# Three edits of order in a fused attention, MLP and soft-MoE kernel: slot sums one step later, running sums behind the exponentials, splits behind the copy of the global keys

## The chip, the cores and the metric

The kernel runs on one core of a Trainium2 chip. The metric is device microseconds of one execution, as the median of several runs. Engines are named as in the profile: PE is TensorE (PEld its weight loads), DVE is VectorE, ACT is ScalarE, POOL is GpSimd, SP is SyncE, whose queue issues the DMAs. A line such as L587 is line 587 of the kernel's source.

## The reference, cut to what matters

```python
# attention: B 4, H 8, S 768, D 64; 8 global keys, a local band of 96
scores = scale * q @ k.T + bias            # bias: -slope * distance
scores = where(is_global | is_local, scores, -1e9)
a = exp(scores - max); a = a / (sum(a) + 1e-9)
x = (a @ v)                                # -> 3072 tokens x 512
# MLP
h = x @ w_in                               # 512 x 2048
x = (h * sigmoid(h)) @ w_out               # 2048 x 512
# soft MoE, 8 experts x 4 slots
logits = x @ phi                           # 3072 x 32
d = exp(logits - logits.max(0)); d /= d.sum(0) + 1e-9
slot_input = d.T @ x                       # 32 slots, sums over all 3072 tokens
slot_out = relu(slot_input @ w1[e]) @ w2[e]
c = softmax(logits, 1)
out = c @ slot_out
```

## The kernel before, in words

The 3072 tokens are 24 tiles T of 128, six to a batch entry (t = T % 6). Three tiles make a chunk c, so there are eight chunks. For each chunk TensorE does two long layers: 16 steps f of layer 1 (`l1_step`, L499 to L501) and 12 quarter steps of layer 2 (`l2_part`, L519 to L521). Nearly every operand is kept as a high and a low fp16 part, so that a product takes three matmuls; `hi` (L199 on ACT, L201 on POOL, L203 on DVE) writes a high part and `lo` (L207, L209) a low one.

While chunk c is in these layers, the attention of the next chunk's tiles is fed in between the steps, from a list of items that `other_items` writes out. For a tile T these are: `s_step(T, pr)` for four pairs of heads (scores, L314 or L324; softmax on DVE L329 and ACT L330), `pv_step(T - 1, half)` (probabilities times values, L369), `split(T + 1)` (the high and low parts of the next tile's q, k and v), `load(T + 2)`. `slot_end` deals the items out evenly over the chunk's first 23 of 28 slots, one slot after each step of the layers.

Two places matter here. The first is the keys' ring `kr` of four tiles: after the scores of tile T are done, its first 8 columns are overwritten with the global keys (`hi("P", kr[:, :, :, u, 0:8], kg, 0)`, POOL, 16x8 elements a partition, tiles with 1 <= t < 5), so that the scores of tile T + 1 find them there. The second is the online soft-max over tokens, a chain that runs one chunk behind: `logits` (L541), `slots1` (transpose L555, maximum L557, L558), `slots2` (maximum of all tokens L565, L568 to L573, then `e16`, the exponentials' high part L203 and low part L209) and `slots3`, which sums the tokens into the slots on TensorE (L585, L587, L589), scales the running sums `acc` and `ssum` by `alpha` (L590, L591) and adds (L593, L594). Each is put off by a number of layer steps with `at(lag, ...)`.

In the first stage (to about 160 us) the MLP's weights are also converted from fp32 pieces to two fp16 parts (`conv`: L459, L461, L466, L469, L479, L487); tiles 0 to 5 go there in another layout (`paired`).

The order in which an engine runs its instructions is not the program's: a list scheduler sets it from its own costs, with the program's order as priority and data dependences as bounds. `tc.issue_after(ins)` adds an edge: what the block traces on the engine of `ins` stands behind `ins` on that engine.

Of the kernel before, what the change touches and what calls it, by code (L numbers as in the profile page):

```python
# [12 lines left out]
ALU = mybir.AluOpType  # L13
# [7 lines left out]
NS = NE * SPE  # L21
# [9 lines left out]
NTILE = NT // 128  # L31
# [3 lines left out]
CT, C0 = max(CHUNKS), CHUNKS[0]  # L35
first = [sum(CHUNKS[:c]) for c in range(NCH)]
chunk_of = {first[c] + i: (c, i) for c in range(NCH) for i in range(CHUNKS[c])}
# [8 lines left out]
def p2(e):  # L46
    return float(2.0 ** e)
# [44 lines left out]
XTE = 'VDA'  # L92
GLE = 'VVVVVVVVVVVVVVVV'
GATE = {1: (0, 0), 2: (0, 1), 3: (1, 0), 4: (1, 1), 5: (2, 0), 6: (2, 1)}
CFG = dict(phi="P", plo="P", xhi="A", xlo="P", ghi="A", lag_l=5, lag_s=2, tail_slots=5)
C4E = "PPPPPPPP"
CTE = "AVAVAVAV"

# [1 line left out]
def fast_kernel(tc, keepp, q_l, k_l, v_l, q_f, k_f, n_global, n_local, w_in, w_out, phi, w1, w2, shapes, pick_c, out):  # L100


    nc = tc.nc
    V, A, G = nc.vector, nc.scalar, nc.gpsimd
# [4 lines left out]
    with ExitStack() as ctx:  # L109
# [87 lines left out]
        def hi(eng, out, in_, e):  # L197
            if eng == "A":
                A.activation(out=out, in_=in_, func=AF.Copy, scale=p2(e))  # L199
            elif eng == "P":  # L200
                G.tensor_scalar(out=out, in0=in_, scalar1=p2(e), scalar2=0.0, op0=ALU.mult, op1=ALU.add)  # L201
            else:
                V.tensor_scalar(out=out, in0=in_, scalar1=p2(e), scalar2=None, op0=ALU.mult)  # L203

        def lo(eng, out, in_, e, h):
            if e == 0:
                (V if eng == "V" else G).tensor_tensor(out=out, in0=in_, in1=h, op=ALU.subtract)  # L207
            else:
                V.scalar_tensor_tensor(out=out, in0=in_, scalar=p2(e), in1=h, op0=ALU.mult, op1=ALU.subtract)  # L209

        def absmax(col, in_, axis=AX.X):
            V.tensor_reduce(out=smp[:, col:col + 1], in_=in_, axis=axis, op=ALU.max, apply_absolute_value=True)
# [26 lines left out]
        def at(lag, fn):  # L239
            seq[0] += 1  # L240
            heapq.heappush(heap, (now[0] + lag, seq[0], fn))
# [5 lines left out]


        staged = {}

        def paired(T):

            return T < NPAIR
# [15 lines left out]
        def split(T):  # L269
# [21 lines left out]
            if t == 2:  # L291
                absmax(T // TPB, v16[:, u, 0:2, 0], AX.XY)

        def s_step(T, pr):
            t, u = T % TPB, T % NR
            w = 128 if t == 0 else 256
# [34 lines left out]
            if pr == 3 and 1 <= t < TPB - 1:  # L331
                if paired(T):
                    hi("P", kr32[:, 0, 0:4, u, 0:8], kg32, 0)
                else:
                    hi("P", kr[:, :, :, u, 0:8], kg, 0)
            if lp == 1:
                pb, ptb = p16[half], pt[half].rearrange("p z h s c -> p (z h s) c")
                if t == 0:
# [18 lines left out]
        def pv_step(T, half):  # L357
# [13 lines left out]
            if half == 1:  # L371
                if 1 <= t < TPB - 1:
                    if paired(T):
                        V.tensor_copy(out=v16[0:8, u], in_=vg[0:8])
                    else:
                        hi("P", v16[0:8, u], vg[0:8], 0)
                if t == TPB - 2 and T + 2 < NTILE:
                    hi("P", vg[0:8], v16[0:8, (T + 2) % NR], 0)
                ri = rinv[T % 2]
                V.tensor_scalar(out=ri, in0=psum_[T % 2], scalar1=1e-9, scalar2=None, op0=ALU.add)  # L380
                V.reciprocal(out=ri, in_=ri)
                V.tensor_tensor(out=x1f, in0=o, in1=ri.rearrange("p (h o) -> p h o", o=1).to_broadcast([128, H, D]), op=ALU.mult)
                xb = x16[T % 2]
                x1v = x1f.rearrange("p h d -> p (h d)")
                c, i = chunk_of[T]
                xv = xt[c][:, :, :, 128 * i:128 * i + 128]
                if T < C0 and XTE[T] != "D":
                    flip(xv[:, 0], xv[:, 1], x1v, XTE[T])
                else:
                    hi(CFG["xhi"], xb[:, 0], x1v, 0)  # L390
                    lo("V" if paired(T) else CFG["xlo"], xb[:, 1], x1v, 0, xb[:, 0])
                    nc.sync.dma_start_transpose(out=xv.rearrange("p z c t -> p (z c) t"), in_=xb.rearrange("p z f -> p (z f)"))

        def first_items():
            items = []
# [17 lines left out]
        def other_items():  # L413
            items, mark = [], {}
            for T in range(C0, NTILE):
# [2 lines left out]
                    items.append(lambda T=T: pv_step(T - 1, 0))  # L418
                items.append(lambda T=T: s_step(T, 1))
                if T + 1 < NTILE:  # L420
                    items.append(lambda T=T: split(T + 1))
                if T + 2 < NTILE and not paired(T + 2):
                    items.append(lambda T=T: load(T + 2, stage_m))
                items.append(lambda T=T: s_step(T, 2))
                if T > C0:
                    items.append(lambda T=T: pv_step(T - 1, 1))
                    mark[T - 1] = len(items)
                items.append(lambda T=T: s_step(T, 3))
                if paired(T + 2):
                    items.append(lambda T=T: load(T + 2, None))  # L430
            items.append(lambda: pv_step(NTILE - 1, 0))
            items.append(lambda: pv_step(NTILE - 1, 1))
            mark[NTILE - 1] = len(items)
            return items, [0] + [mark[first[c] + CHUNKS[c] - 1] for c in range(1, NCH)]

# [125 lines left out]
        def slots2(c):  # L561
# [10 lines left out]
            A.activation(out=l, in_=l, func=AF.Exp)  # L572
            A.activation(out=alpha, in_=alpha, func=AF.Exp)  # L573
            hi("V", e16[:, 0:nt, 0], l, E_E)
            lo("V", e16[:, 0:nt, 1], l, E_E, e16[:, 0:nt, 0])
            at(CFG["lag_s"], lambda: slots3(c))

        def slots3(c):
            nt = CHUNKS[c]
# [7 lines left out]
                        mm(both[:, k], w, e16[:, m], start=(i == 0), stop=(i == 2 * nt - 1))  # L587
            for m in range(nt):
                mm(both[:, 4], ones16, e16[:, m], start=(m == 0), stop=(m == nt - 1))  # L589
            V.tensor_tensor(out=acc, in0=acc, in1=alpha.rearrange("p (o s) -> p o s", o=1).to_broadcast([128, 4, NS]), op=ALU.mult)  # L590
            V.tensor_tensor(out=ssum, in0=ssum, in1=alpha, op=ALU.mult)  # L591
            for y in range(2):
                V.tensor_tensor(out=acc, in0=acc, in1=both[:, 0:4, y], op=ALU.add)  # L593
                V.tensor_tensor(out=ssum, in0=ssum, in1=both[:, 4, y], op=ALU.add)  # L594
# [722 lines left out]
```

## Time and profile before

| | |
|---|---|
| median of 3 runs | 744.09 us (741.79 to 746.35) |
| the profiled execution's own time | 742.64 us |
| its span, first to last instruction | 740.9 us |
| granted TensorE clock, mean | 0.983 |
| busy: PE, DVE, ACT, POOL | 682.3, 463.2, 325.4, 236.5 us |
| DMA | 120.07 MB, mean 162 GB/s |

Busy times are sums over the span; an engine's share says little by itself, since the stages differ. TensorE is the engine that is nearly always busy, so a microsecond in which it waits is read first, then who ended that wait. Matmul rows overlap: the distance from one row's start to the next is the time that it takes from the engine, the row's own duration is longer.

### The profile page before, as it was taken

How to read it: one execution, taken by the hardware profiler on the slowest of the kernel's cores; microseconds unless marked ns; L12 is line 12 of the kernel's file. 1: busy time of each engine (PE TensorE's matmuls, PEld its weight loads, DVE VectorE, ACT ScalarE, POOL GpSimd, SP SyncE). 2: the span in 40 equal slices, each digit the busy share in tenths (PEclk: the TensorE clock that was granted, in tenths of full speed). 3: DMA queues.
4: the chain of work that ended last, by engine and by line, in shares of the span. 5: the costliest groups of instructions: out<-in, count | busy, mean ns of one | idle time of the engine just before them, and what ended most of it. 6: DMA issues, size and time to landing. Idle time of an engine off the chain costs nothing.

```text
span 740.9 us, 13574 instructions
## 1 busy us (share of the span) xinstructions
PE 682.3 (92%) x5175; PEld 390.1 (53%) x5175; DVE 463.2 (63%) x1143; ACT 325.4 (44%) x864; POOL 236.5 (32%) x215
## 2 busy tenths in 40 slices
PE   3789888799999999999999899999999999999993
PEld 2445443345645655566556555665566545665352
DVE  4999889986852887288528872786277216504232
ACT  6868665545522553165215531653155214302121
POOL 0000104530561567135716572356143400300000
PEclk9999898999999999999999999999999999999997
DMA  6998667833563656544635656445224794384997
GB/s 205 270 283 261 138 140 191 268 121 75 108 150 75 110 130 136 121 86 114 143 72 119 125 126 131 86 104 125 58 44 66 172 332 145 124 350 188 380 366 245
DMA packets 165240, 120.07 MB, mean 162 GB/s; under 512 B 143920, under 2 KB 150448, under 8 KB 159152
## 3 DMA queue, kind: packets, MB, share of 16 engines
q1 hardware_dynamic: 165168, 119.13, 60.3%
q8 instruction: 42, 0.69, 0.4%
q14 instruction: 30, 0.25, 0.1%
HBM read 79.01 MB, written 6.29 MB: 115 GB/s over the span
## 4 chain that ended last, share of the span: by engine, by line


## 5 line engine op out<-in xcount | busy, mean ns | idle before, releaser
L201 POOL TENSOR_SCALAR arena<-arena 128x1024 f16<-128x1024 f32 (+5 forms) x127 | 124.3, 991 | 291.1 <-ACT arena L330 111.5
L499 PE MATMUL bank<-rows,arena 128*128 128x384 f16 x512 | 169.1, 331 | 0.8 <-ACT rows L199 0.7
L500 PE MATMUL bank<-rows,arena 128*128 128x384 f16 x512 | 168.9, 330 | 0.0
L501 PE MATMUL bank<-rows,arena 128*128 128x384 f16 x512 | 168.4, 330 | 0.0
L199 ACT ACTIVATE arena<-bank 128x384 f16<-128x384 f32 (+1 forms) x153 | 77.4, 506 | 170.5 <-DVE bank L505 98.2
L330 ACT ACTIVATE arena<-arena 128x256 f32<-128x256 f32 (+1 forms) x192 | 92.2, 482 | 94.9 <-DVE arena L329 93.9
L519 PE MATMUL bank<-arena 128*128 128x512 f16 x336 | 127.0, 383 | 1.9 <-ACT arena L479 1.9
L520 PE MATMUL bank<-arena 128*128 128x512 f16 x336 | 127.6, 380 | 0.5 <-DVE arena L487 0.5
L521 PE MATMUL bank<-arena 128*128 128x512 f16 x336 | 127.5, 380 | 0.0
L209 DVE SCALAR_TENSOR_TENSOR arena<-bank,arena 128x384 f16<-128x384 f32 (+2 forms) x154 | 87.9, 571 | 31.8 <-ACT arena L199 30.7
L207 POOL TENSOR_TENSOR arena<-arena 128x1024 f16<-128x1024 f32 (+1 forms) x45 | 89.7, 1993 | 19.7 <-ACT arena L199 16.7
L329 DVE CUSTOM_DVE_ANT_0 arena<-bank,arena 128x256 f32<-128x256 f32 (+1 forms) x192 | 70.4, 395 | 40.6 <-PE bank L324 36.8
L505 DVE SCALAR_TENSOR_TENSOR bank<-arena,bank 128x384 f32<-128x384 f32 x128 | 71.4, 558 | 32.1 <-ACT arena L503 30.9
L207 DVE TENSOR_TENSOR arena<-arena 128x1024 f16<-128x1024 f32 (+2 forms) x50 | 66.4, 1327 | 14.4 <-POOL arena L201 11.8
L503 ACT ACTIVATE arena<-bank 128x384 f32<-128x384 f32 x128 | 61.8, 483 | 20.0 <-PE bank L501 19.7
L501 PEld LDWEIGHTS <-arena 128*128 128x128 f16 x512 | 50.5, 99 | 34.3 <-issue 1.5
L499 PEld LDWEIGHTS <-arena 128*128 128x128 f16 x512 | 50.7, 99 | 31.3 <-issue 3.6
L500 PEld LDWEIGHTS <-arena 128*128 128x128 f16 x512 | 50.6, 99 | 29.9 <-issue 2.8
L521 PEld LDWEIGHTS <-arena 128*128 128x128 f16 x336 | 32.9, 98 | 39.8 <-issue 0.7
L519 PEld LDWEIGHTS <-arena 128*128 128x128 f16 x336 | 33.0, 99 | 37.4 <-issue 3.6
L520 PEld LDWEIGHTS <-arena 128*128 128x128 f16 x336 | 32.9, 98 | 35.0 <-issue 0.7
L369 PEld LDWEIGHTS <-arena 128*128 128x128 f16 x1056 | 40.1, 102 | 15.6 <-DMA arena<-arena 7.2
(178 smaller groups left out, 786.2 us busy)
## 6 DMA issues: line engine op xcount, KB each, us to landing
arena<-in_w_dram SPq DMA_DIRECT2D x31, 1024.0 KB, 8.4
arena<-in_k_l_dram SPq DMA_DIRECT2D x18, 512.0 KB, 4.3
arena<-in_q_l_dram SPq DMA_DIRECT2D x18, 512.0 KB, 4.1
arena<-in_w_in_dram SPq DMA_DIRECT2D x8, 1024.0 KB, 5.7
arena<-in_w_out_dram SPq DMA_DIRECT2D x8, 1024.0 KB, 5.7
arena<-in_v_l_dram SPq DMA_DIRECT2D x24, 256.0 KB, 3.0
out_dram<-arena SPq DMA_DIRECT2D x6, 768.0 KB, 4.6
arena<-in_q_f_dram SPq DMA_DIRECT2D x6, 256.0 KB, 4.7
```

Of the source, the lines that this page charges most:

```text
L199: A.activation(out=out, in_=in_, func=AF.Copy, scale=p2(e))
L201: G.tensor_scalar(out=out, in0=in_, scalar1=p2(e), scalar2=0.0, op0=ALU.mult, op1=ALU.add)
L207: (V if eng == "V" else G).tensor_tensor(out=out, in0=in_, in1=h, op=ALU.subtract)
L209: V.scalar_tensor_tensor(out=out, in0=in_, scalar=p2(e), in1=h, op0=ALU.mult, op1=ALU.subtract)
L330: A.activation(out=pw, in_=pw, func=AF.Exp, scale=-1.0, bias=nmx[:, T, h:h + 1], accum_out=psum_[T % 2][:, h:h + 1])
L499: mm(hp, wh, x[:, 0, k], start=(k == 0), stop=False)
L500: mm(hp, wh, x[:, 1, k], start=False, stop=False)
L501: mm(hp, wl, x[:, 0, k], start=False, stop=(k == 3))
L505: V.scalar_tensor_tensor(out=hp, in0=th, scalar=1.0, in1=hp, op0=ALU.add, op1=ALU.mult)
L519: mm(op, gh, woh[:, f, 0], start=(f == 0), stop=False)
L520: mm(op, gh, woh[:, f, 1], start=False, stop=False)
L521: mm(op, gl, woh[:, f, 0], start=False, stop=(f == 15))
```

## The change

`slots3` is put off by three layer steps in place of two (`lag_a`); the two DVE scalings of the running sums are queued behind the low part of the exponentials; on POOL, x's low part (tiles from 6 on) and all that `split` traces there are queued behind the latest traced copy of the global keys; x's low part and its transposing DMA become an item of their own, `pv_rest`, behind `s_step(T, 3)`.

```diff
-CFG = dict(..., lag_l=5, lag_s=2, tail_slots=5)
+CFG = dict(..., lag_l=5, lag_s=2, lag_a=3, tail_slots=5)
...
+        glob_part, slot_part = [None], [None]
+        def behind_glob():
+            return tc.issue_after(glob_part[0].ins) if glob_part[0] is not None else ExitStack()
...
+        def split_behind(T):
+            with behind_glob():
+                split(T)
...
-                    hi("P", kr[:, :, :, u, 0:8], kg, 0)
+                    glob_part[0] = hi("P", kr[:, :, :, u, 0:8], kg, 0)
...
                     hi(CFG["xhi"], xb[:, 0], x1v, 0)
-                    lo("V" if paired(T) else CFG["xlo"], xb[:, 1], x1v, 0, xb[:, 0])
-                    nc.sync.dma_start_transpose(out=xv..., in_=xb...)
+                    if paired(T):
+                        pv_rest(T)
+        def pv_rest(T):
+            c, i = chunk_of[T]
+            xb, x1v, xv = ...
+            with behind_glob():
+                lo("V" if paired(T) else CFG["xlo"], xb[:, 1], x1v, 0, xb[:, 0])
+            nc.sync.dma_start_transpose(out=xv..., in_=xb...)
...
-                    items.append(lambda T=T: split(T + 1))
+                    items.append(lambda T=T: split_behind(T + 1))
...
                     items.append(lambda T=T: pv_step(T - 1, 1))
+                items.append(lambda T=T: s_step(T, 3))
+                if T > C0:
+                    if not paired(T - 1):
+                        items.append(lambda T=T: pv_rest(T - 1))
                     mark[T - 1] = len(items)
-                items.append(lambda T=T: s_step(T, 3))
...
-            lo("V", e16[:, 0:nt, 1], l, E_E, e16[:, 0:nt, 0])
-            at(CFG["lag_s"], lambda: slots3(c))
+            slot_part[0] = lo("V", e16[:, 0:nt, 1], l, E_E, e16[:, 0:nt, 0])
+            at(CFG["lag_a"], lambda: slots3(c))
...
-            V.tensor_tensor(out=acc, in0=acc, in1=alpha..., op=ALU.mult)
-            V.tensor_tensor(out=ssum, in0=ssum, in1=alpha, op=ALU.mult)
+            with tc.issue_after(slot_part[0].ins):
+                V.tensor_tensor(out=acc, in0=acc, in1=alpha..., op=ALU.mult)
+                V.tensor_tensor(out=ssum, in0=ssum, in1=alpha, op=ALU.mult)
```

No instruction is added or taken away; a chunk in the middle has 27 items in place of 24 for its 23 slots, and its list now ends behind `s_step(T, 3)` of the next chunk's first tile. On TensorE, from chunk 2 to 5, the matmul L565 and the slot sums had steps f = 8 and 9 of layer 1 between them, with one score block and one block of probabilities times values; now it is f = 8, 9 and 10 with the same two blocks. In chunks 1, 6 and 7 too one step of layer 1 more stands there. The score blocks of pair 3 of one tile and pair 0 of the next had one step of the layers between them, and now have two.

First place: POOL, around the copy of the global keys in the middle of the kernel. 128x16x8 is that copy, 128x8x128 the high part of k, 128x8x64 that of v, 8x1024 the copy of the global values, L207 128x512 x's low part, L207 128x1024 the probabilities' low part; of the rows L201 128x1024 the first behind the copy of the global keys is the high part of q, and the next that of the probabilities. Before:

```order
L201 TENSOR_SCALAR arena<-arena 8x1024
L207 TENSOR_TENSOR arena<-arena 128x512
L201 TENSOR_SCALAR arena<-arena 128x8x128
L201 TENSOR_SCALAR arena<-arena 128x16x8
L201 TENSOR_SCALAR arena<-arena 128x1024
```

Now:

```order
L201 TENSOR_SCALAR arena<-arena 8x1024
L201 TENSOR_SCALAR arena<-arena 128x16x8
L207 TENSOR_TENSOR arena<-arena 128x512
L201 TENSOR_SCALAR arena<-arena 128x1024
L201 TENSOR_SCALAR arena<-arena 128x8x128
L201 TENSOR_SCALAR arena<-arena 128x1024
L201 TENSOR_SCALAR arena<-arena 128x8x64
L207 TENSOR_TENSOR arena<-arena 128x1024
```

The copy of the global keys has moved ahead of x's low part and of k's high part; the high part of q, which had only the copy directly ahead of it, now has the copy and x's low part ahead.

Second place: DVE, in front of the exponentials' low part in chunk 4. L568 (L588 of the new source) are the three maxima behind TensorE's L565, L571 (L591 new) the subtraction ahead of the exponentials, L203 and L209 128x3x32 their high and low part, L209 128x8x64 v's low part, L590 and L591 (L611 and L612 new) the scalings of the running sums. Before:

```order
L569 TENSOR_TENSOR arena<-arena 128x32
L571 TENSOR_TENSOR arena<-arena 128x96
L209 SCALAR_TENSOR_TENSOR arena<-arena 128x8x64
L203 TENSOR_SCALAR arena<-arena 128x3x32
L590 TENSOR_TENSOR arena<-arena 128x128
L209 SCALAR_TENSOR_TENSOR arena<-arena 128x3x32
```

Now:

```order
L589 TENSOR_TENSOR arena<-arena 128x32
L591 TENSOR_TENSOR arena<-arena 128x96
L209 SCALAR_TENSOR_TENSOR arena<-bank_73,arena 128x384
L338 ISA arena<-bank_70,arena 128x256
L338 ISA arena 128x1
L203 TENSOR_SCALAR arena<-arena 128x3x32
L209 SCALAR_TENSOR_TENSOR arena<-arena 128x8x64
L209 SCALAR_TENSOR_TENSOR arena<-arena 128x3x32
L525 SCALAR_TENSOR_TENSOR bank_74<-arena,bank_74 128x384
L611 TENSOR_TENSOR arena<-arena 128x128
L612 TENSOR_TENSOR arena<-arena 128x32
```

The scalings have gone behind the low part, and a layer 1 low part and a softmax pass (L338, L329 before) have come in ahead of it.

Third place: DVE, a little earlier in the same chunk, ahead of the three maxima. L207 64x1024 is q's low part and L207 128x8x128 k's, both of tile 18; L505 (L525 new) and L209 128x384 belong to layer 1. Before:

```order
L329 ISA arena<-bank_70,arena 128x256
L329 ISA arena 128x1
L209 SCALAR_TENSOR_TENSOR arena<-bank_75,arena 128x384
L568 TENSOR_TENSOR arena<-bank_77,arena 128x32 x2
L505 SCALAR_TENSOR_TENSOR bank_76<-arena,bank_76 128x384
```

Now:

```order
L338 ISA arena<-bank_71,arena 128x256
L338 ISA arena 128x1
L207 TENSOR_TENSOR arena<-arena 64x1024
L209 SCALAR_TENSOR_TENSOR arena<-bank_75,arena 128x384
L525 SCALAR_TENSOR_TENSOR bank_76<-arena,bank_76 128x384
L588 TENSOR_TENSOR arena<-bank_77,arena 128x32
L207 TENSOR_TENSOR arena<-arena 128x8x128
L209 SCALAR_TENSOR_TENSOR arena<-bank_76,arena 128x384
```

The low parts of the next tile's q and k now stand directly ahead of and among the maxima; they wait for the high parts that POOL writes in the first place's row.

## Rows read from the trace of the kernel before

**Rows 1.** Waits of PE, whole span: who ended them, us in total, times, longest.

```profile
PE bank L587 <- DVE arena L209: 6.5, 4, 1.9
...
PE bank L324 <- POOL arena L201: 1.6, 1, 1.6
```

**Rows 2.** Busy time by stretch: PE, PEld, DVE, ACT, POOL, then PEclk, DMA share, GB/s.

```profile
320.00:380.00 60.00, 58.54 (x463) 34.67 (x461) 41.08 (x106) 27.19 (x79) 30.10 (x23) 1.00 0.52 113
```

**Rows 3.** PE in order of time, the slot sums: start, us, [idle before <- who ended it].

```profile
263.37 0.19 PE L587 MATMUL bank<-arena 128*128 128x64 f16 x1 [1.69 <-DVE arena L209]
...
405.04 0.36 PE L565 MATMUL bank<-arena 96*128 96x96 f32 x2
...
412.36 0.19 PE L587 MATMUL bank<-arena 128*128 128x64 f16 x1 [1.92 <-DVE arena L209]
```

**Rows 4.** DVE in order of time, from the maxima to the exponentials' low part.

```profile
406.71 0.40 DVE L568 TENSOR_TENSOR arena<-bank,arena 128x32 f32<-128x32 f32 x2
...
408.12 0.68 DVE L382 TENSOR_TENSOR arena<-bank,arena 128x512 f32<-128x512 f32 x1
...
410.22 1.08 DVE L590 TENSOR_TENSOR arena<-arena 128x128 f32<-128x128 f32 x1
411.22 1.09 DVE L209 SCALAR_TENSOR_TENSOR arena<-arena 128x96 f16<-128x96 f32 x1
...
556.52 0.28 DVE L590 TENSOR_TENSOR arena<-arena 128x128 f32<-128x128 f32 x1
556.72 0.25 DVE L209 SCALAR_TENSOR_TENSOR arena<-arena 128x96 f16<-128x96 f32 x1
```

**Rows 5.** PE in order of time, one step of layer 1 between two blocks of logits.

```profile
171.07 0.32 PE L499 MATMUL bank<-rows,arena 128*128 128x384 f16 x1
...
173.01 0.38 PE L541 MATMUL bank<-arena 128*128 128x64 f16 x8
```

**Rows 6.** PE in order of time, the score block that waits for POOL.

```profile
208.87 0.60 PE L324 MATMUL bank<-arena 128*128 128x256 f16 x4 [1.59 <-POOL arena L201]
```

**Rows 7.** POOL in order of time, around copies of the global keys.

```profile
205.96 1.58 POOL L207 TENSOR_TENSOR arena<-arena 128x512 f16<-128x512 f32 x1 [2.67 <-ACT arena L199]
207.52 4.29 POOL L201 TENSOR_SCALAR arena<-arena 128x1024 f16<-128x1024 f32 x4
...
409.55 1.60 POOL L207 TENSOR_TENSOR arena<-arena 128x512 f16<-128x512 f32 x1 [1.82 <-ACT arena L199]
```

**Rows 8.** POOL and DVE by line and shape: times, busy us, mean ns.

```profile
L201 POOL TENSOR_SCALAR arena<-arena 128x1024 f16<-128x1024 f32 x66 | 81.9, 1244 | 159.5 <-ACT arena L330 89.4 <-PE bank L324 47.2 <-issue 12.0
L207 POOL TENSOR_TENSOR arena<-arena 128x512 f16<-128x512 f32 x15 | 20.4, 1357 | 17.2 <-ACT arena L199 16.7
L201 POOL TENSOR_SCALAR arena<-arena 128x128 f16<-128x128 f16 x15 | 4.4, 296 | 22.2 <-PE bank L324 15.0 <-DVE arena L207 7.2
L207 DVE TENSOR_TENSOR arena<-arena 64x1024 f16<-64x1024 f32 x18 | 27.0, 1502 | 4.1 <-POOL arena L201 3.7
```

**Rows 9.** DVE in order of time, a softmax pass, layer 1's and q's low part.

```profile
390.22 0.42 DVE L329 CUSTOM_DVE_ANT_0 arena<-bank,arena 128x256 f32<-128x256 f32 x1
...
390.56 0.56 DVE L209 SCALAR_TENSOR_TENSOR arena<-bank,arena 128x384 f16<-128x384 f32 x1
391.56 1.22 DVE L207 TENSOR_TENSOR arena<-arena 64x1024 f16<-64x1024 f32 x1 [0.44 <-POOL arena L201]
```

**Rows 10.** PE in order of time, waits that ended with a DMA.

```profile
170.84 0.39 PE L541 MATMUL bank<-arena 128*128 128x64 f16 x8 [1.51 <-DMA arena<-arena]
...
598.10 0.87 PE L369 MATMUL bank<-arena 128*128 128x64 f16 x24 [0.80 <-DMA arena<-arena]
```

**Rows 11.** PE in order of time, a wait in the weight conversion.

```profile
115.08 0.61 PE L466 MATMUL bank<-arena 128*32 128x512 bf16 x2 [3.36 <-DVE arena L381]
```

**Rows 12.** Two stretches of the weight conversion, columns as in rows 2.

```profile
88.00:92.00 4.00, 3.94 (x20) 1.95 (x21) 3.49 (x9) 2.31 (x8) 0.18 (x1) 0.51 0.34 86
...
112.00:116.00 4.00, 0.92 (x3) 0.23 (x4) 4.00 (x8) 1.39 (x2) 4.00 (x3) 0.50 0.12 45
```

More of the change, by code (lines that the diff above doesn't have):

```diff
@@ L94 @@
 GATE = {1: (0, 0), 2: (0, 1), 3: (1, 0), 4: (1, 1), 5: (2, 0), 6: (2, 1)}
-CFG = dict(phi="P", plo="P", xhi="A", xlo="P", ghi="A", lag_l=5, lag_s=2, tail_slots=5)
+CFG = dict(phi="P", plo="P", xhi="A", xlo="P", ghi="A", lag_l=5, lag_s=2, lag_a=3, tail_slots=5)
 C4E = "PPPPPPPP"
@@ L200, in hi @@
             elif eng == "P":
-                G.tensor_scalar(out=out, in0=in_, scalar1=p2(e), scalar2=0.0, op0=ALU.mult, op1=ALU.add)
+                return G.tensor_scalar(out=out, in0=in_, scalar1=p2(e), scalar2=0.0, op0=ALU.mult, op1=ALU.add)
             else:
@@ L208, in lo @@
             else:
-                V.scalar_tensor_tensor(out=out, in0=in_, scalar=p2(e), in1=h, op0=ALU.mult, op1=ALU.subtract)
+                return V.scalar_tensor_tensor(out=out, in0=in_, scalar=p2(e), in1=h, op0=ALU.mult, op1=ALU.subtract)
         def absmax(col, in_, axis=AX.X):
@@ L390, in pv_step @@
                     hi(CFG["xhi"], xb[:, 0], x1v, 0)
-                    lo("V" if paired(T) else CFG["xlo"], xb[:, 1], x1v, 0, xb[:, 0])
-                    nc.sync.dma_start_transpose(out=xv.rearrange("p z c t -> p (z c) t"), in_=xb.rearrange("p z f -> p (z f)"))
+                    if paired(T):
+                        pv_rest(T)
+        def pv_rest(T):
+            c, i = chunk_of[T]
+            xb, x1v, xv = x16[T % 2], x1f.rearrange("p h d -> p (h d)"), xt[c][:, :, :, 128 * i:128 * i + 128]
+            with behind_glob():
+                lo("V" if paired(T) else CFG["xlo"], xb[:, 1], x1v, 0, xb[:, 0])
+            nc.sync.dma_start_transpose(out=xv.rearrange("p z c t -> p (z c) t"), in_=xb.rearrange("p z f -> p (z f)"))
         def first_items():
@@ L432, in other_items @@
             items.append(lambda: pv_step(NTILE - 1, 1))
+            items.append(lambda: pv_rest(NTILE - 1))
             mark[NTILE - 1] = len(items)
@@ L589, in slots3 @@
                 mm(both[:, 4], ones16, e16[:, m], start=(m == 0), stop=(m == nt - 1))
-            V.tensor_tensor(out=acc, in0=acc, in1=alpha.rearrange("p (o s) -> p o s", o=1).to_broadcast([128, 4, NS]), op=ALU.mult)
-            V.tensor_tensor(out=ssum, in0=ssum, in1=alpha, op=ALU.mult)
+            with tc.issue_after(slot_part[0].ins):
+                V.tensor_tensor(out=acc, in0=acc, in1=alpha.rearrange("p (o s) -> p o s", o=1).to_broadcast([128, 4, NS]), op=ALU.mult)
+                V.tensor_tensor(out=ssum, in0=ssum, in1=alpha, op=ALU.mult)
             for y in range(2):
```

## The prediction

> **What bounds the kernel now.** I read the waits of TensorE over the whole span first, since it is the engine that nearly always works, then its rows in order of time around each wait, and only then the engines that ended the waits. From about 160 us to 680 us TensorE is the bound: in a stretch from the middle it is busy 58.54 of 60 us, while DVE has 41.08, ACT 27.19 and POOL 30.10 [rows 2]. What is lost there has names: the slot sums L587 wait for the exponentials' low part on DVE 6.5 us in four goes, and one score block L324 waits 1.6 us for POOL [rows 1]. The first stage, with the weights' conversion, is another matter: TensorE waits for DVE there, which has no gap (4.00 of 4 us) [rows 12].
>
> The reader should see in the third group that the slot sums of chunk 4 were wanted at 412.36 - 1.92 = 410.44 us, 5.40 us after L565 started at 405.04, and could start only at 412.36 [rows 3]. The DVE rows say why: from L568 at 406.71 to the end of the low part at 411.22 + 1.09 = 412.31 us DVE runs without a long gap, and a scaling of the running sums (L590, 1.08 us), which nobody waits for yet, lies right ahead of that low part [rows 4].
>
> **The slot sums put off by one step, and the scalings behind the low part.** One step of layer 1 is 173.01 - 171.07 = 1.94 us [rows 5]. It now lies between L565 and the slot sums, so they are wanted 5.40 + 1.94 = 7.34 us after L565. Nothing is added: TensorE does that step anyway. If the low part ended where it ends now, 412.31 - 405.04 = 7.27 us after L565, the wait would be gone by the step alone, and the scaling behind it would give another 1.0 us of room. So the edit itself is worth up to 6.5 us. But the order on DVE has changed with it, and I count that chain anew.
>
> In the new order the score block of pair 3 stands one step ahead of L565, so it ends 1.94 us before L565 starts. It releases POOL's copy of the global keys: 0.30 us. Behind that x's low part, 1.36 us by its mean, and q's high part, 1.24 us by the mean of its shape [rows 8]. That puts the end of q's high part at -1.94 + 0.30 + 1.36 + 1.24 = about 1.0 us after L565. On DVE q's low part stands ahead of the three maxima and needs that high part; queued behind it are two layer 1 operations, the maxima, k's low part and the exponentials, and TensorE's slot sums wait for the last of these. DVE should have run dry meanwhile. That such a wait happens is in the trace: q's low part waited 0.44 us for POOL at 391.56 us [rows 9], with only the copy directly ahead of q's high part; x's low part now comes on top.
>
> q's low part takes 1.22 us [rows 9] and so ends at 2.2 us, or at 2.5 with the mean of 1.50 us [rows 8]. Two layer 1 operations of 0.56 us follow [rows 9]; rows that follow each other overlap by about 0.1 us, so from start to start they are 0.47 us each. The first maximum then starts 3.1 to 3.4 us after L565; before it was 406.71 - 405.04 = 1.67 us. From there to the end of the low part it was 412.31 - 406.71 = 5.60 us. Out of that go L590 (1.00 from start to start), L382 (0.68, so 0.60) and the low part's own excess: 1.09 us beside POOL's x low part, which ran from 409.55 us with four more POOL operations behind it, against 0.25 us alone [rows 4, 7]. In come k's low part (as many elements a partition as q's, so 1.13), one layer 1 low part (0.47) and two softmax passes (0.42, so 0.34 each) [rows 9]: 5.60 - 2.44 + 2.28 = 5.44 us. The low part ends 8.5 to 8.8 us after L565, 1.2 to 1.5 us later than it is wanted. The 5.60 us hold some 0.4 us of gaps that k's low part would fill, which makes it 0.8 at best; with the low part slowed to 1.09 us again it is 2.0 to 2.3. I take a wait of **1.1 us** in place of 6.5 / 4 = 1.63, in four chunks: a gain of 4 x 0.53 = **2.1 us**, between 6.5 (the chain is short after all) and a loss of 4 x 0.67 = 2.7. I take a value near the persisting wait because every length in the chain has a row.
>
> Sharing between DVE and POOL is the weakest item. The trace shows L590 at 0.28 us alone and at 1.08 us beside POOL's operations [rows 4]. [...]
>
> **The copy of the global keys first.** The score block at 208.87 us waited 1.59 us [rows 6] for a copy behind x's low part, which ran from 205.96 us, and among the four operations from 207.52 us [rows 7]. Now the copy comes first on POOL, and two steps (3.9 us) lie between the blocks. That wait goes: **1.6 us**. The price: x's low part now waits for the score block. Its transposing DMA, and on SP's queue the loads and transposes behind it, move with it by a step at most; the next chunk's layer 1 reads x five quarter steps of layer 2 later, which covers it. Uncovered, each chunk would pay the 1.94 us of a step; I cost it at nothing. The probabilities' low part also moves back behind x's, q's, k's and v's parts on POOL, by about 1.36 + 0.7 us; its transposed copy is read some six steps later, so again nothing, and 2 us a tile if that cover were gone.
>
> **The items dealt out anew.** The last tile's second values' block L369, which waited 0.80 us for a DMA at 598.10 us, now stands four quarter steps of layer 2 behind its scores in place of three and a quarter: **0.8 us**. The three transposes ahead of the first logits no longer have a load of v directly ahead on SP's queue; L541 waited 1.51 us there [rows 10]; I take **0.5** between 0 and 1.5. In the conversion stage the order on all engines is reshuffled; DVE has the same work ahead of the last converted piece to within two softmax passes, so I take 0, with 3 us either way.
>
> **Sum.** 2.1 + 1.6 + 0.8 + 0.5 = 5.0 us. The profiled execution took 742.64 us, which gives 737.6; the median shown is 1.45 us higher, so the forecast is **739.1 us**, 0.7% faster.
>
> **The rivals.** *The slot sums' wait is gone.* For it: with the step alone the old chain would have been in time, and three of the seven slot sums wait for nothing today. Against it: the sum above. It gives 6.5 + 1.6 + 0.8 + 0.5 = 9.4 us less, **734.7**.
>
> *It does not do what it says: the wait stays as long*, because DVE now waits for q's high part instead. Gain 1.6 + 0.8 + 0.5 = 2.9: **741.2**, up to 743.9 with the 2.7 us loss. For it: the 0.44 us row; against it: DVE is idle while POOL writes x's low part and q's high part, so both can be shorter than their means, in which DVE's own work slows them.
>
> [...]
>
> **How the numbers follow.** Forecast 0.43 (its own range 736.7 to 741), wait gone 0.26, wait stays 0.19, slower 0.12. Faster by over 1%, which is below 736.65 us and about what a measurement of this kernel can tell from no change, is nearly all of the second case and a little of the first: 0.29. Slower by over 1% is two or three gaps in the conversion: 0.06. Within 1%: 0.65. The range goes from 734, which leaves out the better half of the second case, to 745, which takes in one gap and leaves out the rest: about 0.8 inside.
>
> **What would show it.** Right: L324 has no wait for POOL; L587 keeps three or four waits of about 1 us; ahead of them q's low part on DVE has an idle of 1 to 2 us ended by POOL's L201; L590's successor lies behind the low part. The second case shows L587 gone from TensorE's list. The conversion is right if TensorE's granted clock falls as often before 160 us as it did. Wrong would be a new wait of layer 1 for x, of L369 for a DMA in each tile, or a conversion stage that ends 4 us or more elsewhere than at 160 us.

## The result: 750.03 us against 743.56 us, slower

The changed kernel takes a median of 750.03 us (nine runs, 747.80 to 756.06) against 743.56 us for the kernel before on the same chip (nine, 740.65 to 746.47): 1.0100 times as long, 95% interval 1.0067 to 1.0133. The forecast was 739.1 us, the range 734 to 745. The direction was wrong, and the time lies outside the range. The profiled execution took 749.75 us with a span of 748.0 (before: 742.64 and 740.9).

Lines move with the edit: L324 is now L333, L369 is L378, L541 is L561, L565 is L585, L568 is L588, L587 is L607, L590 and L591 are L611 and L612, the loads are L271, the transposing DMAs of the probabilities, of x and of x2 are L356, L407/L408 and L552.

TensorE's waits over the whole span, the groups that answer to [rows 1] (who waited for whom, us, times, longest):

```profile
PE bank L607 <- DVE arena L209: 8.1, 4, 2.0
...
PE bank L561 <- DMA arena<-arena: 6.1, 3, 2.3
PE bank L378 <- DMA arena<-arena: 5.5, 4, 2.0
```

The scores' wait for POOL is gone from the list, as forecast. The slot sums, which were to lose 2.1 of their 6.5 us, now wait 8.1. The logits, which waited 0.8 us behind the conversion before, wait 6.1. Two of the places, TensorE in order of time ([rows 3] has the second one before):

```profile
387.00 0.39 PE L561 MATMUL bank<-arena 128*128 128x64 f16 x8 [2.28 <-DMA arena<-arena]
...
417.36 0.19 PE L607 MATMUL bank<-arena 128*128 128x64 f16 x1 [2.03 <-DVE arena L209]
```

These waits also cost clock. Stretches of the changed kernel's middle, columns as in [rows 2] (the granted clock is the third figure from the end); before, it was 1.00 in every stretch from 184 to 620 us:

```profile
380.00:440.00 60.00, 55.69 (x454) 33.89 (x453) 40.66 (x104) 26.46 (x75) 29.43 (x23) 0.94 0.48 111
...
388.00:392.00 4.00, 4.00 (x18) 2.15 (x16) 1.32 (x4) 1.09 (x4) 0.00 (x0) 0.58 0.34 66
416.00:420.00 4.00, 2.64 (x36) 1.82 (x36) 3.92 (x17) 2.34 (x6) 0.00 (x0) 0.83 0.92 179
420.00:424.00 4.00, 4.00 (x20) 2.15 (x19) 2.31 (x7) 1.59 (x5) 2.06 (x2) 0.74 0.41 155
```

TensorE is full in 388 to 392 us, yet the clock is 0.58: in quarters of a microsecond it is 0.50 from 388.00 to 391.25 us, and layer 1's matmuls start 0.32 us apart there, against 0.16 us at 1.00: 4 x 0.42 = 1.7 us lost. Three such falls, one in the stretch from 388 us, one from 416 to 424 us and one from 492 to 500 us, lose 5.1 us.

**Where the 7.1 us of span come from.** L565/L585, the slot step's first matmul, marks the chunks: the first of them stood at 183.77 us, the seventh at 625.63; now at 180.17 and 632.72, and the part behind it is the same length (115.3 us). So the conversion stage gained 3.6 us and the chunks lost 10.7. By rows: slot sums +1.6, logits 6.1 - 0.8 = +5.3, clock +5.1, scores' wait -1.6, a wait of the last tile's block of values for a DMA +0.5 (1.27 us at 600.10 us, 0.80 before), together +10.9.

**The slot sums.** VectorE, then GpSimd, ahead of the wait at 417.36 us:

```profile
408.75 2.05 DVE L207 TENSOR_TENSOR arena<-arena 64x1024 f16<-64x1024 f32 x1 [1.12 <-POOL arena L201]
...
411.76 0.18 DVE L588 TENSOR_TENSOR arena<-bank,arena 128x32 f32<-128x32 f32 x1
411.86 1.49 DVE L207 TENSOR_TENSOR arena<-arena 128x1024 f16<-128x1024 f32 x1
...
416.46 0.85 DVE L209 SCALAR_TENSOR_TENSOR arena<-arena 128x512 f16<-128x512 f32 x2
...
406.54 1.16 POOL L207 TENSOR_TENSOR arena<-arena 128x512 f16<-128x512 f32 x1
407.67 4.62 POOL L201 TENSOR_SCALAR arena<-arena 128x1024 f16<-128x1024 f32 x4
```

The second of GpSimd's four operations by itself, k's high part:

```profile
408.68 1.05 POOL L201 TENSOR_SCALAR arena<-arena 128x1024 f16<-128x1024 f32 x1
```

q's low part waits for GpSimd, as forecast, and starts 408.75 - 407.98 = 0.77 us after L585 (forecast 1.0), but takes 2.05 us, not 1.22 to 1.50: it started 0.07 us behind k's high part on GpSimd and ended 1.07 us after that ended. The row at 416.46 us holds two operations: v's low part, which stood ahead of the exponentials' high part before, and behind it the exponentials' low part that TensorE waits for.

**The logits.** VectorE with the low part of x2, GpSimd, then SP's queue, ahead of the wait at 387.00 us, changed kernel:

```profile
378.06 0.68 DVE L209 SCALAR_TENSOR_TENSOR arena<-bank,arena 128x512 f16<-128x512 f32 x1
...
378.59 2.12 POOL L207 TENSOR_TENSOR arena<-arena 128x1024 f16<-128x1024 f32 x1
...
380.73 2.97 SPq L356 DMA_TRANSPOSE arena<-arena  x1
383.75 1.30 SPq L552 DMA_TRANSPOSE arena<-arena  x1
385.15 0.53 SPq L271 DMA_DIRECT2D arena<-in_v_l_dram  x1
388.47 1.23 SPq L552 DMA_TRANSPOSE arena<-arena  x1
```

and the same place of the kernel before:

```profile
376.70 0.69 DVE L209 SCALAR_TENSOR_TENSOR arena<-bank,arena 128x512 f16<-128x512 f32 x1
...
376.66 1.23 SPq L392 DMA_TRANSPOSE rows<-rows  x1
377.94 1.34 SPq L532 DMA_TRANSPOSE arena<-arena  x1
```

The probabilities' transpose can be issued only when their low part on GpSimd ends (378.59 + 2.12 = 380.71 us). x2's transpose, for which the logits wait, stands behind it and goes at 383.75, 5.8 us later than before. Its own input was not what was late: x2's low part ended at 378.74 us (before 377.39), so the transpose stood 5.0 us for its place on the queue, 0.55 before. TensorE wanted the logits at 387.00 - 2.28 = 384.72 us.

**The conversion stage.** The gaps of 3.36 us at 115 us [rows 11] and of 3.04 us at 148.39 us are closed; the longest between 90 and 175 us is now 2.03 us. Between 20 and 184 us the granted clock fell twice in place of three times; four-microsecond stretches times (1 - clock) make 5.1 us of loss against 8.6. That this gave the 3.6 us is not shown: in e1 and e12 below the same sum is 15.4 and 13.7 us, and their first slot step stands at 183.4 and 182.5 us, no later than before. The stretch in which it was lowest now, to set beside [rows 12]:

```profile
136.00:140.00 4.00, 3.79 (x9) 1.28 (x9) 4.00 (x8) 0.50 (x2) 3.66 (x3) 0.50 0.68 242
```

### The profile page after: what moved, and what is told of

Read it like the earlier page. It is cut to its first block, busy times and chain, and to the rows that moved or that the text cites. A ratio compares the mean times of both kernels' runs of the same rounds, so it can differ in the third digit from the quotient of the medians.

```text
span 748.0 us, 13566 instructions
## 1 busy us (share of the span) xinstructions
PE 687.5 (92%) x5175; PEld 391.0 (52%) x5175; DVE 462.6 (62%) x1143; ACT 328.7 (44%) x864; POOL 241.6 (32%) x215
## 4 chain that ended last, share of the span: by engine, by line
## 5 line engine op out<-in xcount | busy, mean ns | idle before, releaser
L201 POOL TENSOR_SCALAR arena<-arena 128x1024 f16<-128x1024 f32 (+5 forms) x127 | 133.3, 1062 | 322.4 <-ACT arena L339 164.8
L541 PE MATMUL bank<-arena 128*128 128x512 f16 x336 | 128.6, 383 | 0.0
L209 DVE SCALAR_TENSOR_TENSOR arena<-bank,arena 128x384 f16<-128x384 f32 (+2 forms) x154 | 87.9, 571 | 43.2 <-ACT arena L199 42.5
L525 DVE SCALAR_TENSOR_TENSOR bank<-arena,bank 128x384 f32<-128x384 f32 x128 | 71.8, 561 | 41.4 <-ACT arena L523 40.1
L207 POOL TENSOR_TENSOR arena<-arena 128x1024 f16<-128x1024 f32 (+1 forms) x45 | 87.4, 1943 | 13.8 <-ACT arena L199 11.7
L207 DVE TENSOR_TENSOR arena<-arena 128x1024 f16<-128x1024 f32 (+2 forms) x50 | 77.4, 1549 | 20.5 <-POOL arena L201 16.2
L338 DVE CUSTOM_DVE_ANT_0 arena<-bank,arena 128x256 f32<-128x256 f32 (+1 forms) x192 | 70.2, 394 | 23.6 <-PE bank L333 20.8
L541 PEld LDWEIGHTS <-arena 128*128 128x128 f16 x336 | 33.1, 99 | 43.9 <-issue 5.3
L378 PEld LDWEIGHTS <-arena 128*128 128x128 f16 x1056 | 39.3, 101 | 18.7 <-DMA arena<-arena 9.1
```

The costliest lines, as they stand in the source:

```text
L201: return G.tensor_scalar(out=out, in0=in_, scalar1=p2(e), scalar2=0.0, op0=ALU.mult, op1=ALU.add)
L209: return V.scalar_tensor_tensor(out=out, in0=in_, scalar=p2(e), in1=h, op0=ALU.mult, op1=ALU.subtract)
L525: V.scalar_tensor_tensor(out=hp, in0=th, scalar=1.0, in1=hp, op0=ALU.add, op1=ALU.mult)
L541: mm(op, gl, woh[:, f, 0], start=False, stop=(f == 15))
```

## Experiments

The theory after the result (A): GpSimd's work behind the copy of the global keys makes the slot sums and the probabilities' transpose late. Rivals: the new dealing of items with x's DMAs (B), the slot step's own edits (C). The experiments ran in four groups, each on one chip (e1 to e4, e5 to e8, e9 to e11, e12), on which the kernel before took 741.1 to 741.8 us; each ratio is to the kernel before on the same chip. In the table "start" is the slot step of the first chunk, "length" from there to the slot step of the seventh, then what of that length TensorE's waits and the falls of the clock took (waits of under 0.5 us left out where they are no group; clock: 4 us stretches times 1 - granted clock).

| kernel | ratio to before, 95% | start | length | slot sums | logits | scores for POOL | clock |
|---|---|---|---|---|---|---|---|
| before | 1 | 183.8 | 441.9 | 6.5 | 0.8 | 1.6 | 0 |
| changed | 1.0100 (1.0067 to 1.0133) | 180.2 | 452.6 | 8.1 | 6.1 | 0 | 5.1 |
| e1 slot step alone | 1.0013 (0.9992 to 1.0034) | 183.4 | 442.5 | 0 | 0 | 5.3 | 1.7 |
| e2 all but slot step | 1.0205 (1.0162 to 1.0248) | 180.4 | 460.8 | 13.4 | 6.2 | 0 | 8.5 |
| e3 no orders behind copy | 1.0058 (1.0033 to 1.0082) | 185.3 | 440.9 | 5.4 | 1.9 | 0 | 0 |
| e4 logits six steps | 0.9901 (0.9871 to 0.9932) | 181.7 | 440.7 | 0 | 0.7 | 0 | 1.7 |
| e5 x2 from ScalarE's queue | 1.0352 (1.0314 to 1.0389) | 186.0 | 467.9 | 11.7 | 10.1 | 0 | 13.7 |
| e6 before, logits six | 0.9976 (0.9952 to 1.0000) | 178.8 | 443.8 | 0 | 0 | 7.5 | 0 |
| e7 as e3, logits six | 0.9924 (0.9898 to 0.9950) | 186.4 | 434.3 | 0 | 0 | 0 | 0 |
| e8 only split behind | 1.0086 (1.0055 to 1.0116) | 183.1 | 449.5 | 8.4 | 2.8 | 0 | 5.1 |
| e9 only x behind | 1.0164 (1.0137 to 1.0191) | 186.3 | 452.4 | 5.7 | 9.5 | 0 | 5.1 |
| e10 as e7, x of one tile behind | 0.9902 (0.9878 to 0.9927) | 184.7 | 434.3 | 0 | 0 | 0 | 0 |
| e11 as e10, old slot step | 1.0024 (1.0004 to 1.0045) | 183.7 | 444.0 | 7.6 | 0.9 | 0 | 0 |
| e12 as e10, splits to tile 10 behind | 0.9888 (0.9859 to 0.9917) | 182.5 | 438.1 | 0 | 0 | 2.4 | 0 |

In e4 3.8 us more are two waits of layer 1 for VectorE, in e12 1.1 us one. Length less all these losses is 432 to 436.5 us in all fourteen kernels, where the lengths themselves differ by 33.6 us: these waits and the clock behind them make nearly all of the difference in the chunks. Not in the columns is a wait of the last tile's block of values for a DMA, 0.8 to 3.2 us, which every kernel has once.

Start, length and waits come from one execution of each kernel. Executions of one kernel differ in their mean granted clock, 0.967 to 0.981 for the nine of the changed kernel, of which the profiled one is the highest; so the number of falls is that of the execution shown.

**e1, the slot step's edits alone in the kernel before** (`lag_a=3`, the scalings behind the low part):

```diff
-            at(CFG["lag_s"], lambda: slots3(c))
+            at(CFG["lag_a"], lambda: slots3(c))
...
+            with tc.issue_after(slot_part[0].ins):
```

> The kernel before with only the two edits of the slot step: its sums three steps behind the exponentials and its running sums scaled behind the exponentials' low part. GpSimd, the items and the DMA queue stay as before. Theory A (the part of the change that queues GpSimd's work behind the copy of the global keys is what costs): the slot sums' wait, 1.63 us at each of four chunks before, falls to 0 to 0.6, no wait of the logits for DMA and no fall of the granted clock appears between 200 and 620 us: 737 to 740 us. Rival C (the new order of the slot step itself brings the waits and the falls of the clock): the waits of the slot sums stay at 2 us, the time is 745 to 750. If one wait of a microsecond or two less gives back no time, 742 to 744.

742.03 us. The slot sums' wait went to nothing, so rival C is wrong; but no time came back. The scores' wait for the copy of the global keys took 3.7 of the 6.5 us; the rest went to the last tile's block of values, which waited 3.15 us for a DMA (0.80 before), with a fall of the clock behind it (1.7 us). e1's group for the scores' line, one more than L324, and that block's row:

```profile
PE bank L325 <- POOL arena L201: 5.3, 5, 2.0
...
597.80 1.46 PE L370 MATMUL bank<-arena 128*128 128x64 f16 x24 [3.15 <-DMA arena<-arena]
```

**e2, the changed kernel without the slot step's edits:**

```diff
-CFG = dict(..., lag_a=3, ...)
+CFG = dict(..., lag_a=2, ...)
...
-            with tc.issue_after(slot_part[0].ins):
+            with ExitStack():
```

> The changed kernel with the slot sums two steps behind and the scalings free again; only the work behind the copy of the global keys and the new items are left. Theory A: the logits' waits for DMA stay (6.1 us in three), the slot sums come one step (74 us of a chunk over 28 steps, 2.6 us) sooner than in the changed kernel while the low part that they read is as late, so they wait 3.5 to 5 us at each of four chunks in place of 2.0: 753 to 760 us. Rival C (the slot step's order costs): 743 to 746 us, waits of the slot sums near 1.6.

757.78 us, as A has it. The slot sums waited 2.75 to 2.93 us in four chunks and 2.04 us in a fifth, less than the 3.5 to 5 expected (I had taken a step at a 28th of a chunk; layer 1's is 1.94 us [rows 5]), and the clock fell five times.

**e3, the changed kernel without its two orders behind the copy:**

```diff
-            return tc.issue_after(glob_part[0].ins) if glob_part[0] is not None else ExitStack()
+            return ExitStack()
```

> The changed kernel without its two orders behind the copy of the global keys: items, place of x's low part and of its DMAs and the slot step as in the changed kernel. TensorE's order is the changed kernel's word for word. Theory A: the slot sums' wait falls from 2.0 to 0 to 0.6 us, the logits' waits for DMA from 6.1 us to at most 2, the clock stays at full speed between 200 and 620 us; the wait of tile scores for GpSimd comes back (1.6 us): 733 to 738 us. Rival B (the dealing of 27 items in place of 24 and x's DMAs behind the probabilities' DMA, not GpSimd's order, cost): the logits' waits stay at 4 to 6 us, 744 to 750 us.

745.44 us: A's time was missed, B's was met. The rows agree with neither as put: in the chunks the logits wait 1.9 us, not 4 to 6, no clock falls, and the 11.7 us that the chunks are shorter than in the changed kernel belong to the orders, as A says. But the slot sums still wait 1.4 us each, and the conversion stage is 5.1 us longer, with a wait of 3.85 us of the logits for a DMA at 171.06 us. (The profiled execution was the fastest of e3's ten, 2.3 us below their median, so its rows stand for the shape, not for the last two microseconds.) VectorE at the place shown above, e3:

```profile
407.33 1.30 DVE L207 TENSOR_TENSOR arena<-arena 64x1024 f16<-64x1024 f32 x1 [1.24 <-POOL arena L201]
...
414.62 0.24 DVE L203 TENSOR_SCALAR arena<-arena 128x96 f16<-128x96 f32 x1
414.79 0.18 DVE L390 RECIPROCAL arena<-arena 128x8 f32<-128x8 f32 x1
414.90 0.26 DVE L209 SCALAR_TENSOR_TENSOR arena<-arena 128x96 f16<-128x96 f32 x1
```

q's low part takes 1.30 us instead of 2.05. It ended at 408.63 us, 1.07 us behind the operation that GpSimd had just begun, which is a short one here:

```profile
407.26 0.30 POOL L201 TENSOR_SCALAR arena<-arena 128x128 f16<-128x128 f16 x1
```

v's low part no longer stands between the exponentials' high and low part, but that did not shorten the chain: from the first maximum to the low part's end it is 5.57 us here and 5.55 us in the changed kernel.

**e4, the logits and all behind them one step later:**

```diff
-CFG = dict(..., lag_l=5, ...)
+CFG = dict(..., lag_l=6, ...)
```

> The changed kernel with a chunk's logits, and the whole slot step behind them, one step later (six in place of five). Theory A with the DMA queue as the cause of the logits' waits: 2.6 us more room makes the three waits for DMA (2.27, 2.28, 1.58 us) vanish, and at least the fall of the clock behind the one at 387 us with them: 740 to 746 us. If the clock falls for another reason than these waits, the 5 us of its falls stay: 744 to 747. If the waits only move on to what comes next: 749 to 752.

734.36 us, better than expected: the logits' waits fell to 0.7 us, and the slot sums' waits, of which I had expected nothing, are gone too, since q's and k's low parts now stand ahead of the maxima. One fall of the clock is left, behind a wait of 2.19 us of layer 1 for VectorE.

**e5, x2's transposes from ScalarE's queue:**

```diff
-            nc.sync.dma_start_transpose(out=xtr, in_=xh...)
+            nc.scalar.dma_start_transpose(out=xtr, in_=xh...)
```

> The changed kernel with x2's transposing DMAs issued from ScalarE's queue in place of SP's; nothing else moves. Theory A (the logits wait since x2's transpose stands on SP's queue behind the probabilities' transpose, which waits for GpSimd's low part): the three waits of the logits for DMA (2.27, 2.28, 1.58 us) fall to 0.5 us together at most, the fall of the clock at 388 us goes with its wait, the slot sums' four waits of 2.0 us and the falls behind them stay: 740 to 744 us. If the DMA itself is late, because of traffic or its inputs, the logits' waits stay at 4 to 6 us: 747 to 752. If ScalarE, which then waits in its own order for VectorE's low part of x2, is what is late, the waits move to matmuls that wait for ScalarE: 748 to 756.

769.14 us, worse than any of the three. SP's queue, ScalarE's queue and TensorE in order of time:

```profile
544.33 1.80 SPq L356 DMA_TRANSPOSE arena<-arena  x1
...
548.68 1.25 ACTq L552 DMA_TRANSPOSE arena<-arena  x1
...
551.79 0.44 PE L561 MATMUL bank<-arena 128*128 128x64 f16 x8 [3.46 <-DMA arena<-arena]
```

and ScalarE's group of waits with its own issue:

```profile
ACT arena L567 <- issue: 56.6, 10, 11.6
```

x2's transpose went out 4.35 us after the probabilities' one; the median of such a DMA on SP's queue, from issue to landing, is 4.3 us, and none of the 21 transposes on ScalarE's queue was in flight together with one of SP's. So here it went out only when the other queue's transpose had landed, where on one queue it followed at once (383.75 us against 380.73 + 2.97 in the changed kernel). ScalarE stood idle ahead of such issues, 56.6 us in all in ten goes; a part of that is the wait for x2's low part, which in the go shown ended at 542.34 us, 3.96 us into an idle of 11.6. So this kernel doesn't test A's queue order: it puts a harder order in its place.

**e6, the kernel before with `lag_l=6`** (the edit of e4 alone).

> The kernel before with nothing but the logits (and the slot step behind them) one step later, six in place of five. If the step of room is a gain of its own, which the change has no part in: the slot sums' 6.5 us and the logits' 2.3 us of waits go, 733 to 737 us against some 742. If it only mends what the change broke (x's and the probabilities' DMAs in front of x2's): 740 to 743 us, with waits of the slot sums that stay or move on to the tile scores as they did with the slot step alone.

740.22 us: the second case. The slot sums' 6.5 us went, and scores for GpSimd waited 7.5 us, as in e1. So of e4's gain the later step alone has a quarter, and by the rows none of it in the chunks: their length is 443.8 us against 441.9, the start is 5.0 us earlier. (This profiled execution was the fastest of twelve, 2.7 us below their median.)

**e7, e3 and e4 together** (no orders, `lag_l=6`).

> The changed kernel with the logits one step later and without its two orders behind the copy of the global keys. If with that step of room the orders cost nothing in the steady part and only help in the stage of the weights' conversion (a wait of 3.85 us of the logits for DMA at 171 us without them, none with them): slower than the same kernel with the orders by 3 to 5 us, 737 to 740 us. If the orders cost the steady part even so: 730 to 733 us.

736.51 us, between the two cases: by the rows both halves are true. The orders cost the chunks 440.7 - 434.3 = 6.4 us even with the later step, and save the conversion stage 186.4 - 181.7 = 4.7 us. The sizes are rough: e4's profiled execution was the slowest of its six and e7's the fastest of its nine, and while these rows make e4 the slower one by 1.7 us, the ratios make it the faster (0.9901 against 0.9924, with intervals that overlap).

**e8, only the split behind the copy:**

```diff
-            with behind_glob():
+            with ExitStack():
                 lo("V" if paired(T) else CFG["xlo"], xb[:, 1], x1v, 0, xb[:, 0])
```

> The changed kernel with x's low part free again; the next tile's split still stands behind the copy of the global keys. If it is the split's parts that make GpSimd's later work late: the slot sums' waits stay at 1.8 to 2.0 us and the logits' at 5 to 6 us in three: 747 to 751 us. If it is x's low part: the waits as without either order (1.4 us; two of about 1 us) and no fall of the clock: 743 to 746 us.

748.47 us. The split makes the slot sums late: they wait 8.4 us, with three falls of the clock. The logits wait less than expected, 2.8 us in the chunks. e8's VectorE and TensorE in order of time:

```profile
411.11 2.05 DVE L207 TENSOR_TENSOR arena<-arena 64x1024 f16<-64x1024 f32 x1 [1.24 <-POOL arena L201]
...
418.82 0.84 DVE L209 SCALAR_TENSOR_TENSOR arena<-arena 128x512 f16<-128x512 f32 x2
...
419.71 0.19 PE L607 MATMUL bank<-arena 128*128 128x64 f16 x1 [2.15 <-DVE arena L209]
```

**e9, only x's low part behind the copy:**

```diff
         def split_behind(T):
-            with behind_glob():
-                split(T)
+            split(T)
```

> The changed kernel with the next tile's split free again; x's low part still stands behind the copy of the global keys (the logits five steps behind, as in the changed kernel). If the split is what makes the slot sums late: their waits fall from 2.0 to 1.3 to 1.5 us, no fall of the clock behind them, and the stage of the conversion keeps its gain (the slot step of the first chunk at 180 to 181 us): 740 to 744 us. If x's low part behind the copy brings the logits' waits for DMA on its own: three waits of some 2.2 us stay, with a fall of the clock behind at least one: 745 to 749 us.

753.69 us, beyond the second case: the logits' waits come with x's low part alone, five in place of three (four of them in the chunks, 9.5 us), and the slot sums are back at 1.3 to 1.55 us. The gain of the conversion stage, which both cases kept, is gone: the first slot step stands at 186.3 us. e9's two groups (its lines are one less):

```profile
PE bank L560 <- DMA arena<-arena: 12.1, 5, 3.3
...
PE bank L606 <- DVE arena L209: 5.7, 4, 1.5
```

**e10, e7 with x's low part of one tile behind the copy:**

```diff
-            with behind_glob():
+            with behind_glob() if T < 7 else ExitStack():
```

> A version made from what the runs showed: the changed kernel with the logits one step later, both orders behind the copy taken away again except for the low part of x of one tile (the seventh), whose two DMAs stood in front of the first chunk's x2 transposes on SP's queue. If this queue place is what cost the conversion stage: the logits' wait of 4.07 us at 171 us falls to 0 to 1.6, and the steady part stays as it is without the orders (434 us from the first slot step to the last but one): 731 to 734 us. If the wait at 171 us comes from the two loads that also stand there, it stays at 3 to 4 us: 735 to 738.

734.51 us. The wait at 171.81 us fell from 4.07 to 2.68 us, between the two cases: x's DMAs were part of it. Two loads still stood ahead of and among x2's three transposes.

**e11, e10 with the slot step of before** (`lag_a=2`, scalings free).

> The version before this one without the two edits of the slot step: its sums two steps behind the exponentials again and the scalings free; GpSimd's order is the same word for word. If with a step of room the slot step's own edits do nothing: the same time within 2 us. If they still take a wait away: the slot sums wait 0.5 to 1.6 us at each of four to seven chunks, 3 to 8 us slower.

743.32 us, 8.8 more than e10, a little above what the second case gave: the slot sums waited 7.6 us. So the slot step's edits, worth nothing in e1, are worth 9 us where no other wait takes their place.

**e12, e10 with the splits of the tiles up to the tenth behind the copy**, which puts the two loads behind x2's transposes:

```diff
-            split(T)
+            with behind_glob() if T < 10 else ExitStack():
+                split(T)
```

> The version with the logits six steps behind and x's low part of one tile behind the copy, and now the splits of the tiles up to the tenth behind the copy too: two loads that stood between the first chunk's x2 transposes on SP's queue come after them; from the fourth chunk on GpSimd's order is the one without the orders. If those loads are what is left of the wait at 171 us (2.68 us): it falls to under 0.5, the slot step of the first chunk starts at 180 to 182 us in place of 184.7, and the steady part keeps its 434 to 436 us: 729 to 733 us. If they are not, 734 to 737; if the split behind the copy costs even in two chunks (slot sums' waits come back there): 736 to 739.

734.01 us. The wait at 171 us is gone and the first slot step starts 2.2 us earlier, but the chunk behind it pays for it (a score block waits 2.35 us for GpSimd at 206.55 us). e4, e10 and e12 are equal within their intervals; the three are 1% faster than before.

## Why the prediction was wrong

**The step that failed** is the one on the moved transposes, "I cost it at nothing", and the sentence behind it on the probabilities' low part, "its transposed copy is read some six steps later, so again nothing". I had named the transposes behind x's on the queue, but asked only when the readers of x and of the probabilities would need them. The DMA that was short of time was a third one on SP's queue: x2's transposes, whose logits come five steps later. The trace of the changed kernel shows them behind the probabilities' transpose with their own input ready 5.0 us before, e9 shows the waits with x's low part alone, e8 without it takes 3.3 us of them away and e3, without either order, 4.2, and e4 shows that one step more is nearly all they lacked. Measured: 5.3 us more of waits where the sum had none. The "2 us a tile if that cover were gone" that I had named was the right size for one wait, but stood in no rival and in no end of the range.

**The slot sums: right mechanism, wrong size.** The term was a wait of 1.1 us; it is 2.03. TensorE wanted them 7.35 us after L585 (forecast 7.34), and the low part ended 9.33 us after it (forecast 8.5 to 8.8, with 2.0 to 2.3 us of wait as the stated end). One length was short: q's low part took 2.05 us where the sum had 1.22 to 1.50, and the first maximum started 3.78 us after L585, not 3.1 to 3.4. From there to the low part's end the sum was right, 5.55 us against 5.44. e3 and e8 show the same: without the split behind the copy q's low part takes 1.30 us and the wait is 1.4 us, with it 2.05 and 2.1. I had charged x's low part for the delay; in e9, with x's low part alone behind the copy, the wait is 1.3 to 1.55 us, so the further 0.5 to 0.7 us is the split's. The second rival, "the wait stays as long", described this part rightly: VectorE waited 1.12 us for q's high part on GpSimd, and q's low part then ended 1.07 us behind GpSimd's k part.

**The clock in the chunks** was left out. The sum has no term for it, as before none of the waits there, up to 1.92 us, had a fall behind it. 5.1 us.

**What held.** The scores' wait of 1.6 us went. The wait at 170.84 us [rows 10] is gone (forecast: 1.0 of its 1.51 us left). The block of values still waits for a DMA, 1.27 us at 600.10 us where it waited 0.80; the gain of 0.8 did not come. The conversion stage gave 3.6 us, a little outside the 3 either way; one fall of the clock fewer goes with it, but e1, with a loss of 15.4 us by the clock there, is no later than the kernel before. So the "slower" of the chances, by gaps in the conversion, did not come. No run shows a price for such a gap, of which the range's end of 745 us takes in one: what the runs show is e1's first slot step at 183.4 us with that loss of 15.4 us, against 183.8 us with 8.6 before.

**Of the change's parts**, the slot step's edits remove their wait, but in the kernel before that wait had hidden others, the scores' wait for GpSimd above all (e1). The orders behind the copy remove the scores' wait, which e3 shows gone by the new items without them as well, and bring the waits for the slot sums and the logits. The gain was there to be had with one step more for the logits (e4).

What stays open: why e9 has five late logits and the changed kernel three; its two further ones in the chunks, of 3.1 and 3.3 us, also have x2's transpose behind the probabilities' on SP's queue (302.23 behind 300.33 us). Not separated is which steps of the conversion stage move its start between 178.8 and 186.4 us; queue places explain the wait at 171 us, the falls of the clock before it differ from kernel to kernel.

## What to carry to other kernels

When a step that ends in a DMA is put off, list what stands behind that DMA on its queue, and compare each reader's slack there, not only the slack of the DMA's own reader: here the reader with the least lag paid. An engine's step that is moved takes its parts on other engines along (the split's q part on VectorE), and they land in somebody's chain. A wait that is removed need not give its time; test such an edit with one more step of room (e1 took 6.5 us of waits away and gave nothing, the same edit from e11 to e10 gave 9 us).

## What was not expected of the hardware

Behind a wait of TensorE the granted clock sometimes fell, and that loss came on top of the wait. In the chunks of all fourteen kernels it fell behind each of the 12 waits of 2.7 to 3.8 us, behind 9 of the 19 waits of 2.0 to 2.4 us, and behind none of the 43 of 1.0 to 1.9 us. A fall lost 1.7 us, three of them, two in e5 and one in e9, 3.4 us. In the changed kernel two waits of 2.02 and 2.04 us cost only themselves, and two of 2.03 and 2.04 us another 1.7 us each.

VectorE's low part of q took 1.22 us at the place of [rows 9], 1.30 in e3 and 2.05 us in the changed kernel and e8. The rows of all fourteen kernels after 180 us say when: in 56 goes no operation of GpSimd was in progress as it started, and it took 1.22 us in each; in 152 goes one was, and in 150 of them it ended 1.07 or 1.08 us after that operation's end, whatever that one's length (1.04 to 2.14 us in the kernel before and the changed one, 0.30 us in the e3 row above). (The two others, one of them that of [rows 9], started within 0.01 us of GpSimd's and took 1.22 us.) So the operation of GpSimd that came next after q's high part set the price of q's low part: 1.05 us of k's high part in the changed kernel, which made it 2.05 us, an operation of 0.30 us in e3, which made it 1.30.
